# Five small moves in a fused sparse-attention and two-layer kernel: two matmul pieces, a deal of pieces, an order of sums, a split addition and a memset

## The chip, the cores and the metric

The kernel runs on one core of one Trainium2 chip. The metric is the device time of one execution in microseconds (us). The engines go by their short names: PE is TensorE, ACT ScalarE, DVE VectorE, POOL GpSimd, and SP is SyncE, which here only issues DMAs. Each engine works through its own list of instructions in order; semaphores order the engines among each other.

## The reference

Eight batches of eight heads, 576 positions, 64 columns per head. Heads 0 to 3 see the last 32 positions (local), heads 4 to 7 every position of the same remainder modulo 32 (strided). The attention output, 4608 rows of 512, goes through two layers.

```python
B, H, S, D = q.shape                                   # 8, 8, 576, 64
scores = scale * np.matmul(q, k.transpose(0, 1, 3, 2))
mask_local = (rel >= 0) & (rel < 32)                   # rel = query position - key position
mask_strided = (rel >= 0) & (pos[None, :] % 32 == pos[:, None] % 32)
scores = np.where(masks, scores, -1e9)                 # heads 0-3 local, 4-7 strided
attn = softmax(scores)
x = np.matmul(attn, v)  ->  [4608, 512]
h = x @ w_in                                           # [512, 2048]
g = np.maximum(h, 0.0) + alpha * np.minimum(h, 0.0)
out = g @ w_out                                        # [2048, 512]
```

## The kernel before, in words

**Attention.** Heads are handled in pairs, 32 in all: pairs 4b and 4b+1 are the local heads of batch b, 4b+2 and 4b+3 the strided ones. A pair goes through pieces: transposes of q and k (`T`, line 292), scores (`score_both`, `score_piece`: matmuls of lines 318 and 377, the exponential on ACT, lines 391 to 406, and a product with the mask on POOL or DVE, lines 397, 402 and 409), the product with v (`pv_piece`: matmuls of line 430, then on DVE a reciprocal and a product, lines 437 and 439), and a transposition of the result into xT, by PE and a copy (`x_piece`, line 455, copies of lines 230 to 234) or by a transposing DMA (`x_dma`, lines 469 and 472, with a copy on ACT, line 478). xT is a ring of 1536 columns with four blocks of 128 rows (kk): kk 0 and 1 hold the local pairs of a batch, kk 2 and 3 the strided ones.

**The two layers.** The 4608 rows are nine chunks of 512. The first layer of a chunk is 16 pieces (`lin1_piece`): four matmuls of 512 columns over kk (line 613), the negative part on ACT (`neg`, line 621), and the join with alpha on DVE (`gT`, line 624), which goes into a list `late` and is written out at the next step. The second layer of chunk 0 is plain: `U(kf)` are three matmuls of 512 columns (line 884), `W(i)` two (line 899), called a quarter piece here. The second layer of chunks 1 to 8 (`lin2_fast`) uses a scheme with seven products, named "1", "5", "6", "2", "7", "3", "4" in their order, on sums of blocks of g (`gsum`, line 653, on POOL or DVE) and of w_out (`wsum`, line 640); each has two parts of eight (or sixteen) matmuls of 256 columns (lines 709 and 719). Their accumulators lie in PSUM banks a, b, e and f; bank b takes products "6", "7" and "4" upon a copy of a. The results go out through `store` (copy on ACT, line 662, or addition on DVE, line 664, then a DMA from SP, line 668). The accumulators and the first layer's outputs share one pool of three PSUM buffers, used in turn.

**Order.** The program order is written out by hand and kept. It begins with loads, memsets and a list of pieces for batch 0 and chunk 0; then a second list (from line 913) mixes U and W with the pieces of batch 1. The scores of pairs 4 and 5 come in it as `sc1(4)` and `sc1(5)`. From then on a loop runs over the chunks n = 1 to 8 with 30 steps each, i = 0 to 15 for the first layer and i = 16 to 29 for the second. After each step `attn_n(cnt, ab)` deals out cnt attention pieces of the next batch. cnt comes from an accumulator that spreads the pieces left over the steps (half as densely in the first layer), except in chunk 1 and chunk 6, which have lists of steps of their own. The dictionaries `early`, `sums`, `sums2` say at which step a gsum is made and by which engine.

**Loads.** SP and ACT issue the first loads of q and k; POOL issues those of v and of the weights, which change the type on the way, through the software queue (q0 of the profile). `x16s` is a fixed tile of 80 rows for the strided pairs that are transposed by DMA; its last 16 rows are set to zero once.

Of the kernel before, what the change touches and what calls it, by code (L numbers as in the profile page):

```python
# [9 lines left out]
F32 = mybir.dt.float32  # L10
F16 = mybir.dt.float16
ALU = mybir.AluOpType
# [20 lines left out]
def kernel(  # L33
# [10 lines left out]
    nc = tc.nc  # L44
    keep = tc.keep_in_program_order
# [443 lines left out]
    def T(u, nm):  # L489
        return lambda: transpose_piece(u, nm)  # L490
# [110 lines left out]
    def lin1_piece(n, m, begin=False):  # L601
        if n not in gTs:
            gTs[n] = gpool.tile([128, 16, 512], F16, tag="gT", name="gT")
        c0 = (512 * n) % RING
        hps = begun.pop(m, None)
        if hps is None:
            pool, tag = (pspool, "ps") if n == 0 and m // 3 % 2 else (phpool, "hps")
            hps = pool.tile([128, 512], F32, tag=tag, name="hps")
            order = (0, 1, 2, 3) if n else (2, 3, 0, 1)
        else:  # L610
            order = (0, 1)
        for kk in order[0:2] if begin else order:
            keep(nc.tensor.matmul(  # L613
                hps, win16[:, kk, 128 * m : 128 * m + 128], xT[:, kk, c0 : c0 + 512],
                start=(kk == (0 if n else 2)), stop=(kk == (3 if n else 1))))
        if begin:
            begun[m] = hps
            return

        neg = npool.tile([128, 512], F32, tag="neg", name="neg")  # L620
        keep(nc.scalar.activation(neg, hps, AF.Relu, scale=-1.0))  # L621

        def fin():
            keep(nc.vector.scalar_tensor_tensor(  # L624
                gTs[n][:, m, :], neg, oma[:, m : m + 1], hps, op0=ALU.mult, op1=ALU.add))
        late.append(fin)
# [45 lines left out]
    def lin2_fast(n, i):  # L672

        last = n == NCH - 1
        x, r = (("1", i) if i < 2 else ("5", i - 2) if i < 4 else ("6", i - 4) if i < 6 else ("2", i - 6) if i < 8
                else ("7", i - 8) if i < 10 else ("3", i - 10) if i < 12 else ("4", i - 12))
        if last and i > 10:  # L680
            x, r = (("4", 0), ("4", 1), ("3", 1))[i - 11]
        b = {"1": "a", "2": "a", "5": "e", "3": "e"}.get(x, "b")
        first = x in "15" and r == 0
        if first:
            bank[b] = phpool.tile([128, 512], F32, tag="hps", name="ops")
        o = bank[b][:, 256 * r : 256 * r + 256]
        if last and b == "e" and r == 1:
            o = bank["f"][:, 0:256]

        def g(t, j):  # L690
            return lambda y: gTs[n][:, 2 * y + j, 256 * t + 128 * r : 256 * t + 128 * r + 128]

        def s(z):
            return lambda y: gsum[z][:, y, 128 * r : 128 * r + 128]

        def w(j, c):
            return lambda y: wout16[:, 2 * y + j, 256 * c : 256 * c + 256]

        def t(z):
            return lambda y: wsum[z][:, y, :]  # L700

        def both(h):
            if x == "5" and h == 0 and last:
                bank["f"] = pspool.tile([128, 512], F32, tag="ps", name="opsl")
            for z in range(2):
                i, alone = int(x) - 5, x == "5" and last and z == 1
                o = bank["f"][:, 0:256] if alone else bank[b][:, 256 * z : 256 * z + 256]
                for y in range(4 * h, 4 * h + 4):
                    keep(nc.tensor.matmul(  # L709
                        o, gsum[i][:, y, 128 * z : 128 * z + 128], wsum[i][:, y, :],  # L710
                        start=(x == "5" and y == 0 and (z == 0 or alone)), stop=(y == 7), skip_group_check=True))

        lhs, rhs = {
            "1": (g(0, 0), w(0, 0)), "2": (g(0, 1), w(1, 0)), "3": (s(3), w(1, 1)),
            "4": (g(1, 1), t(3)), "5": (s(0), t(0)), "6": (s(1), t(1)), "7": (s(2), t(2))}[x]
        if x in "56":
            both(r)
        for y in range(0 if x in "56" else 8):
            keep(nc.tensor.matmul(  # L719
                o, lhs(y), rhs(y), start=(first and y == 0), stop=(y == 7), skip_group_check=True))  # L720
        if last and x == "3":
            store(n, 0, 1, bank["f" if r else "e"], bank["s6"], r)
            return
        if last and x == "5" and r:
            bank["s5"] = npool.tile([128, 512], F32, tag="par", bufs=2, name="par")
            for z, o in enumerate((bank["e"], bank["f"])):
                keep(nc.scalar.copy(bank["s5"][:, 256 * z : 256 * z + 256], o[:, 0:256]))
            return
        if r == 0:
            return  # L730
        if x == "1":
            bank["b"] = phpool.tile([128, 512], F32, tag="hps", name="ops")
            keep(nc.scalar.copy(bank["b"], bank["a"]))
        elif x in "56":
            z = npool.tile([128, 512], F32, tag="par", bufs=2, name="par")
            keep(nc.scalar.copy(z, bank[b]))  # L736
            bank["s" + x] = z
        elif x == "2":
            store(n, 0, 0, bank["a"])
        elif x == "7":  # L740
            late.append(lambda: store(n, 1, 1, bank["b"], bank["s5"]))
        elif x == "3":
            late.append(lambda: store(n, 0, 1, bank["e"], bank["s6"]))
        else:
            store(n, 1, 0, bank["b"])
# [40 lines left out]
    keep(nc.vector.memset(kTs[0][:, :, 608:672], 0.0))  # L786
    for nm in "qk":
        keep(nc.vector.memset(qks[nm][64:80], 0.0))
    keep(nc.vector.memset(x16s[64:80], 0.0))
    keep(nc.vector.tensor_copy(id32, ident[0:72, 0:72]))  # L790

    keep(nc.gpsimd.memset(vss[0][:, :, :, 64:65], 1.0))
# [30 lines left out]
    def ov(b, eng, c0, c1):  # L823
        return lambda: over_v(b, eng, c0, c1)
# [82 lines left out]
    def ws(z):  # L907
        return lambda: wout_sum(z, "dve", 0)

    def sc1(g, eng="dve"):  # L910
        return lambda: score_both(pairs[g], eng)

    for fn in [
        vs(1, 0, "pool"), sc1(6), U(0), vs(1, 1, "pool"), U(1), sc1(7), U(2), U(3), Cl(1, "q", "act"), Pv(6, 1),
        Cl(1, "k"), Pv(6, 2), Pv(6, 0), U(4), U(5), Pv(7, 0), Pv(7, 1), U(6), loads2, T(2, "q"), U(7), Pv(7, 2), W(0), W(1),
        T(2, "k"), ws(0), ws(1), ws(2), W(2), sc1(4), U(8), W(3), ov(1, "dve", 0, 24), U(9), sc1(5, "pool"), W(4), U(10), X(7, "act"), U(11),
        X(6, "act"), Pv(4, 1), W(5), Cl(2, "q", "act"), Cl(2, "k", "act"), U(12), Pv(4, 0), U(13), Pv(5, 0), U(14), Pv(5, 1),
        U(15), W(6), X(4, "dve"), X(5, "dve"), W(7)]:
        fn()
# [18 lines left out]
    for n in range(1, NCH):  # L938
        ab = attn_until(n + 1) if n + 1 < B else len(pieces)
        left = ab - pos["i"]  # L940
        acc = 0.0
        for i in range(30):
            if i < 16:
                lin1_piece(n, 8 * (i // 8) + 2 * (i % 4) + i % 8 // 4)
            else:
                lin2_fast(n, i - 16)
            held = []
            if n == 1 and i == 15:
                held.extend(late)
                late.clear()  # L950
            if n == 6:
                cnt = int(i in (2, 5, 7, 9, 16, 17, 19, 20, 22, 24, 25, 27))
            elif n == 1:
                cnt = int(i > 12 or i in (0, 2, 4, 6, 9, 11))
            else:
                acc += left / (19.5 if n == B - 2 else 21) * (0.5 if i < 16 else 1.0)
                cnt = int(acc)
                acc -= cnt
            attn_n(cnt, ab)
            for fn in held:  # L960
                fn()
            if n == 2 and i == 8:
                load_v(4, True)
            for z, h, eng in {1: early, 2: sums2}.get(n, sums).get(i, ()):
                g_sum(n, z, h, eng)
            if n > 1:
                continue
            if i == 7:
                for pr in range(2):
                    cast_v(2, pr, "pool")  # L970
                    load_qk(4, "qk"[pr])
            if i == 4:
                load_v(3, True)
            if i == 15:
                load_v(3, False)
                load_d(3)
                cast_l(3, "q", "act")
            if i == 17:
                cast_l(3, "k", "act")
            if i == 24:  # L980
                for pr in range(2):
                    cast_v(3, pr, "pool")
        while pos["i"] < ab:
            attn_step(ab)
# [30 lines left out]
```

## Time and profile before

| | before |
|---|---|
| median of 3 runs | 297.91 us (297.36 to 298.34) |
| the profiled execution | 296.76 us |
| its span, first to last instruction | 294.9 us |
| granted TensorE clock | 1.000 |
| PE busy | 289.3 us (98%) |
| DVE busy | 216.1 us (73%) |
| ACT busy | 182.1 us (62%) |
| POOL busy | 181.7 us (62%) |
| HBM read, written | 38.24 MB, 9.44 MB |

A row of the timeline reads: start and duration in us, engine, line, operation, output <- inputs, shapes, xcount, and in brackets the idle time of the engine before it and what ended that. Rows of one line in a stretch are merged, and the duration is that of the merged row. PE's matmuls overlap: each is shown some 0.16 us longer than the step from one to the next. Line numbers are those of the kernel before.

### The profile page before, as it was taken

What the parts mean: (1) busy time and instruction counts of PE and PEld (TensorE: products, weight loads), DVE (VectorE), ACT (ScalarE), POOL (GpSimd) and SP (SyncE); (2) the same over time, 40 slices, a digit from 0 to 9 for tenths busy, and PEclk for the clock granted to TensorE, in tenths of its full rate; (3) what the DMA queues carried; (4) which work ended last, traced back from release to release, by engine and by line L of the source; (5) the groups of instructions that cost most, each with busy time, mean ns of one, the idle gap of its engine ahead of it and who ended that gap; (6) DMA issues with size and microseconds to landing.
All of it is one profiled execution on the core that took longest, in us unless ns stands there. A gap on an engine that the chain in (4) does not pass through costs nothing.

```text
span 294.9 us, 6948 instructions
## 1 busy us (share of the span) xinstructions
PE 289.3 (98%) x2732; PEld 187.3 (64%) x2732; DVE 216.1 (73%) x412; ACT 182.1 (62%) x337; POOL 181.7 (62%) x167
## 2 busy tenths in 40 slices
PE   8999999999999999999999999999999999999995
PEld 3764554545885488547864786478646864784584
DVE  5688876579966895689668975897489948927851
ACT  1777756797957864775477537754776266417630
POOL 8462547999589997889897985777364105002200
PEclk9999999999999999999999999999999999999999
DMA  7999999999999999999999999976411230021004
GB/s 180 263 194 203 239 212 258 221 158 336 114 110 196 153 151 129 195 136 153 174 185 146 122 144 194 134 115 117 150 20 23 58 109 0 0 87 58 2 0 143
DMA packets 97488, 41.18 MB, mean 140 GB/s; under 512 B 75360, under 2 KB 94256, under 8 KB 97456
## 3 DMA queue, kind: packets, MB, share of 16 engines
q0 software_dynamic: 51008, 17.77, 59.7%
q1 hardware_dynamic: 46096, 22.32, 37.2%
q10 hardware_dynamic: 352, 0.66, 0.9%
q8 instruction: 21, 0.34, 0.5%
q14 instruction: 11, 0.09, 0.1%
HBM read 38.24 MB, written 9.44 MB: 162 GB/s over the span
## 4 chain that ended last, share of the span: by engine, by line
PE 91%; DVE 3%; DMA 2%; issue 2%; ACT 1%; SPq 0%; DVEq 0%; ACTq 0%
PE hps L613 41%; PE ops L719 22%; PE ops L709 8%; PE pv L430 5%; PE ops L884 4%; PE sp L377 2%; DMA consts<-consts 2%; PE tp L292 1%; PE xp L455 1%; PE sph L377 1%; PE ops L899 1%; DVE gT L624 1%; PE tf L154 1%; DVE gsum L653 1%; PE wps L761 1%
## 5 line engine op out<-in xcount | busy, mean ns | idle before, releaser
L613 PE MATMUL hps<-xT,win 128*128 128x512 f16 x576 | 132.9, 379 | 0.1
L624 DVE SCALAR_TENSOR_TENSOR gT<-neg,oma,hps 128x512 f16<-128x512 f32 x144 | 105.2, 744 | 36.2 <-ACT neg L621 28.6
L621 ACT ACTIVATE neg<-hps 128x512 f32<-128x512 f32 x144 | 85.8, 598 | 34.6 <-PE hps L613 32.4
L613 PEld LDWEIGHTS <-win 128*128 128x128 f16 x576 | 53.3, 98 | 58.3 <-issue 0.8
L653 POOL TENSOR_TENSOR gsum<-gT 128x1024 f16<-128x1024 f16 x15 | 31.8, 2123 | 37.6 <-DVE gT L624 37.5
L402 POOL TENSOR_TENSOR et<-et,consts 128x576 f16<-128x576 f16 (+1 forms) x23 | 32.1, 1394 | 34.7 <-ACT et L400 34.4
L719 PEld LDWEIGHTS <-gT 128*128 128x128 f16 x384 | 35.7, 98 | 6.1 <-issue 0.5
L439 DVE TENSOR_TENSOR x<-pv,rc 96x384 f16<-96x384 f32 (+2 forms) x62 | 33.0, 532 | 2.1
L719 PE MATMUL ops<-wout,gT 128*128 128x256 f16 x256 | 32.1, 273 | 0.0
L709 PE MATMUL ops<-wsum,gsum 128*128 128x256 f16 x248 | 30.7, 273 | 0.2 <-DVE gsum L653 0.2
L409 POOL TENSOR_TENSOR et<-et,consts 128x576 f16<-128x576 f16 (+1 forms) x23 | 29.7, 1290 | 0.1
L430 PEld LDWEIGHTS <-et 72*128 72x128 f16 (+1 forms) x448 | 23.6, 98 | 8.4 <-ACT et L339 0.4
L709 PEld LDWEIGHTS <-gsum 128*128 128x128 f16 x256 | 23.6, 98 | 3.3 <-DVE gsum L653 0.4
L719 PEld LDWEIGHTS <-gsum 128*128 128x128 f16 x256 | 23.7, 98 | 2.9
L400 ACT ACTIVATE et<-sp 128x576 f16<-128x576 f32 (+1 forms) x24 | 15.5, 645 | 16.4 <-PE sp L377 16.4
L664 DVE TENSOR_TENSOR osb<-ops,par 128x512 f32<-128x512 f32 (+1 forms) x16 | 10.7, 674 | 17.1 <-PE ops L719 9.4
L437 DVE RECIPROCAL rc<-pv 72x6 f32<-72x6 f32 (+2 forms) x80 | 14.7, 183 | 10.2 <-PE pv L430 9.8
L662 ACT COPY osb<-ops 128x512 f32<-128x512 f32 x16 | 9.4, 587 | 16.8 <-PE ops L719 16.7
L406 ACT ACTIVATE et<-sph 128x288 f16<-128x288 f32 (+1 forms) x48 | 18.9, 409 | 0.0
L736 ACT COPY par<-ops 128x512 f32<-128x512 f32 x15 | 8.8, 587 | 13.1 <-PE ops L709 12.6
L719 PE MATMUL ops<-wsum,gT 128*128 128x256 f16 x128 | 16.1, 273 | 0.3 <-DVE osb L664 0.3
L719 PE MATMUL ops<-wsum,gsum 128*128 128x256 f16 x128 | 16.1, 272 | 0.0
(112 smaller groups left out, 354.5 us busy)
## 6 DMA issues: line engine op xcount, KB each, us to landing
out_dram<-osb SPq DMA_DIRECT2D x35, 256.0 KB, 3.0
vl<-in_v_dram POOLq DMA_DIRECT2D x6, 384.0 KB, 9.7
win<-in_moe_w_in_dram POOLq DMA_DIRECT2D x4, 512.0 KB, 17.4
wout<-in_moe_w_out_dram POOLq DMA_DIRECT2D x4, 512.0 KB, 17.1
qsd<-in_q_dram POOLq DMA_DIRECT2D x7, 288.0 KB, 7.5
ksd<-in_k_dram POOLq DMA_DIRECT2D x7, 288.0 KB, 8.8
stv<-in_v_dram POOLq DMA_DIRECT2D x7, 288.0 KB, 7.7
ql<-in_q_dram SPq DMA_DIRECT2D x3, 576.0 KB, 8.8
```

Source lines behind the costliest of these rows:

```text
L400: keep(nc.scalar.activation(ev.rearrange("r (y c) -> r y c", y=2), sp[0:r, :, 0:n], AF.Exp, scale=SCALE))
L402: keep(mul(mv, mv, m, op=ALU.mult))
L406: keep(nc.scalar.activation(ev[:, n * y : n * y + n], sps[y][0:r, 0:n], AF.Exp, scale=SCALE))
L409: keep(mul(mv, mv, m, op=ALU.mult))
L430: keep(nc.tensor.matmul(pv[:, 65 * x : 65 * x + 65], et[0:r, c : c + 128], v16[0:r, 2 * P.pr + hh, t, :] if P.strided else v16[:, 6 * (2 * ...
L439: keep(nc.vector.tensor_tensor(P.x16[0:w, c0 : c0 + 64 * nb].rearrange("r (c e) -> r c e", e=64), pvv[:, :, 0:64], rc[0:w, 0:nb].unsqueeze ...
L613: keep(nc.tensor.matmul(hps, win16[:, kk, 128 * m : 128 * m + 128], xT[:, kk, c0 : c0 + 512], start=(kk == (0 if n else 2)), stop=(kk == ( ...
L621: keep(nc.scalar.activation(neg, hps, AF.Relu, scale=-1.0))
L624: keep(nc.vector.scalar_tensor_tensor(gTs[n][:, m, :], neg, oma[:, m : m + 1], hps, op0=ALU.mult, op1=ALU.add))
L653: keep((nc.vector if eng == "dve" else nc.gpsimd).tensor_tensor(gsum[i][:, hs], a, b, op=op))
L709: keep(nc.tensor.matmul(o, gsum[i][:, y, 128 * z : 128 * z + 128], wsum[i][:, y, :], start=(x == "5" and y == 0 and (z == 0 or alone)), st ...
L719: keep(nc.tensor.matmul(o, lhs(y), rhs(y), start=(first and y == 0), stop=(y == 7), skip_group_check=True))
```

## The change

Five edits, all in the order or place of work; the same matmuls are made.

1. In the second list, `W(3)` moves from behind `U(8)` to ahead of `sc1(4)`, the scores of pair 4.
2. Chunk 6 loses its own list of steps: cnt comes from the accumulator as in chunks 2 to 5. The pieces of its first layer then come at steps 3, 6, 9 and 12 instead of 2, 5, 7 and 9 (in the order: pair 28's second product with v, pair 30's scores, pair 29's two products with v); those from step 16 on stay.
3. `lin1_piece` of chunk 1 sums over kk in the order 2, 3, 0, 1, as chunk 0 does.
4. In the last chunk, product "7" adds its result and s5 in two halves of 256 columns, at once instead of through `late`, with one store for both.
5. The memset of the last 16 rows of `x16s` moves from DVE, as its last but one instruction ahead of the first loads' use, to POOL, ahead of the memsets and DMAs that POOL begins with.

```diff
-            order = (0, 1, 2, 3) if n else (2, 3, 0, 1)
+            order = (0, 1, 2, 3) if n > 1 else (2, 3, 0, 1)
...
-                start=(kk == (0 if n else 2)), stop=(kk == (3 if n else 1))))
+                start=(kk == (0 if n > 1 else 2)), stop=(kk == (3 if n > 1 else 1))))
...
+        elif x == "7" and last:
+            osb = opool.tile([128, 512], F32, tag="osb", name="osb")
+            for z in range(2):
+                c = slice(256 * z, 256 * z + 256)
+                keep(nc.vector.tensor_tensor(osb[:, c], bank["b"][:, c], bank["s5"][:, c], op=ALU.add))
+            keep(nc.sync.dma_start(
+                out[512 * n + 256 : 512 * n + 512, 256:512].rearrange("(r p) c -> p r c", p=128),
+                osb.rearrange("p (r c) -> p r c", r=2)))
         elif x == "7":
             late.append(lambda: store(n, 1, 1, bank["b"], bank["s5"]))
...
-    keep(nc.vector.memset(x16s[64:80], 0.0))
+    keep(nc.gpsimd.memset(x16s[64:80], 0.0))
...
-        T(2, "k"), ws(0), ws(1), ws(2), W(2), sc1(4), U(8), W(3), ov(1, "dve", 0, 24), U(9), ...
+        T(2, "k"), ws(0), ws(1), ws(2), W(2), W(3), sc1(4), U(8), ov(1, "dve", 0, 24), U(9), ...
...
-            if n == 6:
-                cnt = int(i in (2, 5, 7, 9, 16, 17, 19, 20, 22, 24, 25, 27))
-            elif n == 1:
+            if n == 1:
```

More of the change, by code (lines that the diff above doesn't have):

```diff
@@ L915 @@
         Cl(1, "k"), Pv(6, 2), Pv(6, 0), U(4), U(5), Pv(7, 0), Pv(7, 1), U(6), loads2, T(2, "q"), U(7), Pv(7, 2), W(0), W(1),
-        T(2, "k"), ws(0), ws(1), ws(2), W(2), sc1(4), U(8), W(3), ov(1, "dve", 0, 24), U(9), sc1(5, "pool"), W(4), U(10), X(7, "act"), U(11),
+        T(2, "k"), ws(0), ws(1), ws(2), W(2), W(3), sc1(4), U(8), ov(1, "dve", 0, 24), U(9), sc1(5, "pool"), W(4), U(10), X(7, "act"), U(11),
         X(6, "act"), Pv(4, 1), W(5), Cl(2, "q", "act"), Cl(2, "k", "act"), U(12), Pv(4, 0), U(13), Pv(5, 0), U(14), Pv(5, 1),
```

## The prediction

> **What bounds the kernel now.** I read the page first, then the chain that ended last, then each engine's timeline wherever TensorE (PE) stands still for longer than its own matmuls explain. The page and two pieces of the chain:
>
> ```profile
> span 294.9 us, 6948 instructions
> PE 289.3 (98%) x2732; PEld 187.3 (64%) x2732; DVE 216.1 (73%) x412; ACT 182.1 (62%) x337; POOL 181.7 (62%) x167
> ...
> PE 91%; DVE 3%; DMA 2%; issue 2%; ACT 1%; SPq 0%; DVEq 0%; ACTq 0%
> ...
> 72.72 0.87 PE ops L719 x8
> ...
> 88.98 2.59 PE hps L613 x12
> ```
>
> PE is busy for 98% and carries 91% of the chain. Back to back, a 512-column matmul takes 2.59 / 12 = 0.216 us and a 256-column one 0.87 / 8 = 0.109. The change adds and removes no matmul. So it can gain only where PE starts a matmul later than these steps allow, and since PE is dense elsewhere, a hole closed anywhere should move the end by its size. The edits meet five such places.
>
> **The two quarter pieces** (W(3), two 512-column matmuls) move ahead of pair 4's scores. PE and VectorE (DVE) there:
>
> ```profile
> 44.39 0.59 PE L899 MATMUL ops<-wout,gT 128*128 128x512 f16 x2
> 45.46 0.30 PE L377 MATMUL sp<-qT,kT 64*128 64x96 f16 x6 [0.47 <-DVE kT L232]
> ...
> 44.59 0.72 DVE L232 COPY kT<-tp 128x512 f16<-128x512 f16 x1 [0.73 <-PE tp L292]
> ```
>
> W(2) leaves PE free at 44.39 + 2 x 0.216 = 44.82, but the scores start at 45.46, when the copy of kT has ended: a hole of 0.64 (the row's 0.47 counts from the modelled end of the matmul). W(3) is 0.43 of work and needs nothing that W(2) lacked. It fits into the hole, the scores start at 45.46 as before, and everything behind them is 0.43 earlier. The copy hangs on transposes issued before W(2), so nothing is queued behind a new wait. Bounds: 0 to -0.43; I take **-0.43**, for the hole is larger than the work.
>
> **Chunk 1, strided heads first.** The next line-613 group is its first:
>
> ```profile
> 55.44 0.73 PE L613 MATMUL hps<-xT,win 128*128 128x512 f16 x2
> ...
> 54.92 0.82 DVE L232 COPY xT<-xp 128x576 f16<-128x576 f16 x2
> ```
>
> Two matmuls took 0.73, against 0.59 for the two at 44.39: 0.14 more, as the second needs pair 5's xT, copied until 55.74. With kk 2 and 3 first, the local heads are needed 0.43 later, and the copies cover that. Bounds 0 to -0.18; I take **-0.14**.
>
> These 0.57 must survive until chunk 2, where ScalarE (ACT) waits for a transposing DMA:
>
> ```profile
> 87.19 1.40 ACT L478 COPY xT<-xs 128x384 f16<-128x384 f16 x2 [0.16 <-DMA xs<-x16s]
> 88.50 0.69 ACT L230 COPY xT<-xp 128x384 f16<-128x384 f16 x2
> ...
> 88.81 2.75 PE L613 MATMUL hps<-xT,win 128*128 128x512 f16 x12
> ```
>
> PE needs the last copy (ended 89.19) for its fourth matmul, at 88.81 + 3 x 0.216 = 89.46: slack 0.27. If that DMA lands 0.57 earlier like its issuers, nothing is lost: **0**. If it stays where it is, 0.57 - 0.27 = 0.30 comes back; that is the upper bound.
>
> **Chunk 6 by the accumulator.** Pair 28's last piece moves from step 2 to 3, pair 30's scores from 5 to 6, pair 29's pieces from 7 and 9 to 9 and 12; from step 16 on all is equal.
>
> ```profile
> 219.21 5.63 PE L613 MATMUL hps<-xT,win 128*128 128x512 f16 x24
> ...
> 229.89 0.29 PE L430 MATMUL pv<-vs,et 72*128 72x65 f16 x4
> 230.41 1.05 PE L709 MATMUL ops<-wsum,gsum 128*128 128x256 f16 x8 [0.23 <-DVE gsum L653]
> ...
> 226.90 1.76 DVE L653 TENSOR_TENSOR gsum<-gsum,gT 128x1024 f16<-128x1024 f16 x1
> ...
> 229.28 1.07 DVE L653 TENSOR_TENSOR gsum<-gsum,gT 128x1024 f16<-128x1024 f16 x1
> ...
> 226.78 1.34 POOL L402 TENSOR_TENSOR et<-et,consts 72x576 f16<-72x576 f16 x1 [3.74 <-ACT et L400]
> ```
>
> At the usual pace 24 matmuls take 2.75 + 12 x 0.216 = 5.34; here 5.63. The 0.29 is PE waiting for a PSUM buffer, because DVE, given pair 29's two pieces only two steps apart, falls behind with gT. Three steps apart it does not: chunk 5 deals so, and shows what is late next:
>
> ```profile
> 190.82 0.35 PE L430 MATMUL pv<-vl,et 128*128 128x65 f16 x6
> ...
> 193.05 1.39 DVE L624 SCALAR_TENSOR_TENSOR gT<-neg,oma,hps 128x512 f16<-128x512 f32 x2
> ...
> 200.77 1.28 DVE L653 TENSOR_TENSOR gsum<-gT,gsum 128x1024 f16<-128x1024 f16 x2
> ...
> 201.04 2.15 POOL L402 TENSOR_TENSOR et<-et,consts 128x576 f16<-128x576 f16 x1 [3.93 <-ACT et L400]
> ```
>
> There the gT behind the piece ends at 193.05 + 0.69 = 193.74, 2.92 after the piece's matmuls began, and frees a PSUM buffer some 0.1 later. In chunk 6 the first second-layer group wants that buffer 6 x 0.03 + 12 x 0.216 = 2.77 after them: a new hole of 0.25 at step 16 (chunk 5 has pair 27's scores in between, chunk 6 not). So -0.29 + 0.25.
>
> The second hole: the four 65-column matmuls at 229.89, each 65/256 of 0.109, 0.03, end at 230.01, and PE goes on at 230.41: 0.40, for gsum(1,1). DVE is late because a gsum that meets a mask product of GpSimd (POOL) takes 1.76 and 1.07 instead of 1.28 / 2 = 0.64. In chunk 5 the same pair met, DVE had started first, and POOL took 2.15. Whoever starts first keeps its pace. At 226.78 POOL was 0.12 ahead of the gsum at 226.90. The new hole delays pair 31's scores, and with them the mask, by 0.25, but not the gsum: now DVE is first by 0.13, gsum(1,1) ends about 1 us sooner, and the hole goes: -0.40. If the order holds as it was, 0.40 - 0.25 = 0.15 stays. Bounds of this edit: 0 (both holes as before) to -0.69 (no new one); I take **-0.44**.
>
> **The last chunk's addition in halves.**
>
> ```profile
> 287.62 1.04 PE L719 MATMUL ops<-wout,gsum 128*128 128x256 f16 x8
> 288.98 1.91 PE L719 MATMUL ops<-wsum,gT 128*128 128x256 f16 x16 [0.32 <-DVE osb L664]
> ...
> 237.23 0.69 DVE L664 TENSOR_TENSOR osb<-ops,par 128x512 f32<-128x512 f32 x1 [0.58 <-PE ops L719]
> ...
> 288.23 1.02 DVE L664 TENSOR_TENSOR osb<-ops,par 128x512 f32<-128x512 f32 x2 [4.03 <-issue]
> 291.85 0.42 DVE L664 TENSOR_TENSOR osb<-opsl,par 128x256 f32<-128x256 f32 x1 [2.60 <-PE opsl L719]
> ```
>
> PE could go on at 287.62 + 8 x 0.109 = 288.49 and goes on at 288.98: 0.49, because "4" adds into the bank that this addition reads. If half the bank were released after the first half, 0.69 - 0.42 = 0.27 would be won. But in the built program the first half raises no semaphore, the second raises it by 2, and PE's one wait, ahead of "4"'s first half, stands at the count that the second reaches. So PE waits for both. The addition at 288.23 and the 256-column one behind it take 1.02 together, so the second starts 1.02 - 0.42 = 0.60 after the first, 0.09 before its 0.69 is over; two halves end after (0.42 - 0.09) + 0.42 = 0.75, 0.06 later than one: **+0.06**. [...] Bounds: -0.27 to +0.16 (twice 0.42 less 0.69, rounded up). The store follows the second half in either case and lies well ahead of the end.
>
> **The memset of x16s on POOL** stands ahead of all DMAs that POOL issues:
>
> ```profile
> 0.79 0.22 POOL L793 MEMSET vl<- 32x64 f16 x1
> ...
> 1.41 1.55 POOL L212 DMA_DIRECT2D stv<-in_v_dram  x2 [0.25 <-issue]
> ...
> 84.62 2.02 POOL L234 COPY vs<-stv 72x1024 f16<-72x1024 f16 x2
> ...
> 4.49 0.48 DVE L789 MEMSET x16s<- 16x512 uint32 x1
> 6.89 0.19 DVE L790 CAST id<-consts 72x72 f32<-72x72 f16 x1 [1.92 <-DMA consts<-consts]
> 10.12 0.43 DVE L232 COPY vs<-stv 72x1024 f16<-72x1024 f16 x1 [0.32 <-DMA stv<-in_v_dram]
> 10.65 0.46 DVE L232 CAST qT<-tf 128x288 f16<-128x288 f32 x1
> ...
> 11.47 0.30 PE L318 MATMUL sp<-qT,kT 64*128 64x72 f16 x8
> ...
> q10 hardware_dynamic: 291, 0.56, 37.9%
> q1 hardware_dynamic: 321, 0.46, 33.2%
> ...
> q0 software_dynamic: 9, 0.01, 5.4%
> ```
>
> DVE gains nothing: it waits 1.92 for the constants. For POOL the trace has no memset of 1024 columns: 0.22 for 64 columns is the floor, 2.02 for two copies of 1024 makes 1.01 each, twice that the ceiling; I take 1.0. Every issue of POOL, v first, then the weights, is then 1.0 later. The last three rows are the DMA queues in the first 6 us (the first two) and in the seventh: POOL's queue, issued to from 1.41, moved nothing in 6 us while two others shared the engines, and 9 packets in the next. An issue at 2.4 is still well ahead, so the v load lands when it did: **0**. Ceiling: the full delay D, in the rivals.
>
> **Sum.** -0.43 - 0.14 - 0.44 + 0.06 = -0.95. The profiled execution took 296.76, 1.86 more than its span; it becomes 295.8. The median of the runs, 297.91, is 1.15 above it; the same step gives **297.0**.
>
> **Rivals.** (1) The v load moves with its issue, D = 1.0. The copy at 10.12 and, in order behind it, the cast of qT (free to start at 10.65, DVE busy until 10.55 + D) slide; the cast ends at 12.01, the scores of pair 3 start at 12.05 instead of 11.47: +0.58, 297.5. For it: between 10.1 and 11.5 nothing has more slack than the 0.42. Against: the queue rows. [...] Chance 0.15. (2) **Slower**: the same place with a memset at its ceiling, D = 2.0 or more: each further us of D adds 1 us, so the price is D - 0.42. It eats the 0.95 from D = 1.4, at 2.0 it gives 298.5, and passes +0.3% at D = 2.3. Chance 0.09. (3) The transposing DMA of chunk 2 does not move: +0.30, 297.3; for it, ACT's wait at 87.19; against, that all that issues it hangs on PE. Chance 0.13. (4) The halves do release the bank early: -0.33 against the sum, 296.6; chance 0.07. The forecast has 0.56.
>
> A measurement of this kernel tells about 0.3%, 0.89 us, from no change, so faster begins at 297.0: the forecast lies on that edge. Its unknown ends lean outward (no new hole in chunk 6, -0.25), and case 4 lies beyond; I give faster 0.50, same 0.44, slower 0.06. The range: the largest gains together, -0.43 - 0.18 - 0.69 - 0.27, reach 296.3; upwards it takes in cases 1 and 3 and half the spread of the runs shown (0.4), but only part of case 2: 296.2 to 298.3.
>
> **What would show it.** The scores of pair 4 with a hole near 0.2 instead of 0.64; two matmuls in 0.59 at the head of chunk 1; 24 matmuls of chunk 6 without the 0.29, a hole of 0.25 ahead of its first L719 group, gsum at 0.7 beside a longer mask; near 0.55 ahead of the last sixteen L719; the v copy still at 10.1. Wrong it is if that copy moves to 11, if chunk 2's first matmuls spread beyond 2.75, or if the gsums of chunk 6 stay at 1.76.

## The result, and the profile after

| | before | after |
|---|---|---|
| median, 14 runs each | 297.33 us | 296.38 us |
| fastest | 296.98 | 295.57 |
| ratio of after to before, 95% interval | | 0.9967 [0.9952, 0.9982] |
| profiled execution, its span | 296.76, 294.9 | 297.99, 296.2 |

The median fell by 0.95, the sum forecast. It stands at 296.4 and not at the 297.0 named, because the forecast started from three runs of before with a median of 297.91; the fourteen here have 297.33. But the profiled execution of after is one of its three longest: it is *longer* than that of before, and shows both what the edits won and what is lost in some executions. (Runs in a disturbed state are left out of the ratios; the profiles of three experiments, e1, e8 and e13, have a mean clock of 0.994, and of these only distances between neighbouring instructions are used.)

The page of after, lines on the span and the chain:

```profile
span 296.2 us, 6949 instructions
...
PE 80%; DMA 11%; DVE 4%; POOL 2%; ACT 2%; issue 1%; SPq 0%; DVEq 0%; ACTq 0%; POOLq 0%
...
PE hps L613 38%; PE ops L719 20%; PE ops L709 8%; DMA win<-in_moe_w_in_dram 5%; PE ops L892 4%; DMA kT<-ksd 4%; PE pv L430 3%; DMA xs<-x16s 2%; PE sp L377 2%; DVE gsum L653 1%; PE ops L907 1%; PE tp L292 1%; PE sph L377 1%; PE xp L455 1%; D
```

The chain was 2% DMA before and is 11% now: three loads end waits that PE did not have. First the places of the edits, PE unless marked (lines behind 739 are 8 further down than before, those behind 953 6):

```profile
45.08 1.03 PE L907 MATMUL ops<-wout,gT 128*128 128x512 f16 x4
46.15 0.30 PE L377 MATMUL sp<-qT,kT 64*128 64x96 f16 x6
...
55.68 1.03 PE L613 MATMUL hps<-xT,win 128*128 128x512 f16 x4
...
223.72 2.75 PE L613 MATMUL hps<-xT,win 128*128 128x512 f16 x12
226.54 1.03 PE L719 MATMUL ops<-wout,gT 128*128 128x256 f16 x8
...
231.74 0.29 PE L430 MATMUL pv<-vs,et 72*128 72x65 f16 x4
231.87 1.04 PE L709 MATMUL ops<-wsum,gsum 128*128 128x256 f16 x8
...
228.60 0.69 DVE L653 TENSOR_TENSOR gsum<-gsum,gT 128x1024 f16<-128x1024 f16 x1
...
228.63 1.79 POOL L402 TENSOR_TENSOR et<-et,consts 72x576 f16<-72x576 f16 x1 [4.91 <-ACT et L400]
...
289.08 1.04 PE L719 MATMUL ops<-wout,gsum 128*128 128x256 f16 x8
290.20 1.91 PE L719 MATMUL ops<-wsum,gT 128*128 128x256 f16 x16
...
289.33 0.81 DVE L744 TENSOR_TENSOR osb<-ops,par 128x256 f32<-128x256 f32 x2 [3.67 <-issue]
```

Pair 4's scores start 0.21 behind W(3) (45.08 + 4 x 0.216 = 45.94). Four matmuls at the head of chunk 1 take 1.03, so none of them waits. In chunk 6 the first-layer matmuls run without a stall, a hole of 0.23 stands ahead of the first second-layer group (223.72 + 12 x 0.216 = 226.31), and none ahead of the line-709 group (four steps of 0.03 from 231.74). The gsum that took 1.76 takes 0.69, 0.03 ahead of a mask product that now takes 1.79. The last hole is 0.25 (289.08 + 0.87 = 289.95), not 0.49. Won: 0.43 + 0.14 + 0.45 + 0.24 = 1.26 (the expectations below have 0.23 and 1.25).

Lost in this execution, PE and ACT:

```profile
19.35 0.36 PE L430 MATMUL pv<-vl,et 128*128 128x65 f16 x6
20.38 0.60 PE L613 MATMUL hps<-xT,win 128*128 128x512 f16 x2 [0.67 <-DMA win<-in_moe_w_in_dram]
...
71.09 0.30 PE L377 MATMUL sp<-qT,kT 64*128 64x72 f16 x8 [0.84 <-DMA kT<-ksd]
...
89.57 1.40 ACT L478 COPY xT<-xs 128x384 f16<-128x384 f16 x2 [1.53 <-DMA xs<-x16s]
...
89.81 1.12 PE L613 MATMUL hps<-xT,win 128*128 128x512 f16 x3
91.39 1.46 PE L613 MATMUL hps<-xT,win 128*128 128x512 f16 x6 [0.46 <-ACT xT L230]
```

The first weights cost 0.83, the transposing DMA of kT 0.90, that of xs 0.93 (91.39 less 89.81 + 3 x 0.216): 2.66 in all. Besides, PE's first transposes started 0.25 sooner (the cast of the constants is at 6.56 instead of 6.89), and 0.14 of that went into a wait for the first copy of v: 2.66 + 0.14 - 0.25 - 1.26 = 1.29, against 1.3 between the spans.

### The profile page after: what moved, and what is told of

Its sections match the earlier page's. It is cut to its first block, busy times and chain, and to the rows that moved or that the text cites. A ratio compares the mean times of both kernels' runs of the same rounds, so it can differ in the third digit from the quotient of the medians.

```text
span 296.2 us, 6949 instructions
## 1 busy us (share of the span) xinstructions
PE 289.4 (98%) x2732; PEld 187.5 (63%) x2732; DVE 215.2 (73%) x412; ACT 182.3 (62%) x337; POOL 183.1 (62%) x168
## 3 DMA queue, kind: packets, MB, share of 16 engines
q0 software_dynamic: 51008, 17.77, 60.5%
## 4 chain that ended last, share of the span: by engine, by line
PE 80%; DMA 11%; DVE 4%; POOL 2%; ACT 2%; issue 1%; SPq 0%; DVEq 0%; ACTq 0%; POOLq 0%
PE hps L613 38%; PE ops L719 20%; PE ops L709 8%; DMA win<-in_moe_w_in_dram 5%; PE ops L892 4%; DMA kT<-ksd 4%; PE pv L430 3%; DMA xs<-x16s 2%; PE sp L377 2%; DVE gsum L653 1%; PE ops L907 1%; PE tp L292 1%; PE sph L377 1%; PE xp L455 1%; DVE gT L624 1%
## 5 line engine op out<-in xcount | busy, mean ns | idle before, releaser
L664 DVE TENSOR_TENSOR osb<-ops,par 128x512 f32<-128x512 f32 (+1 forms) x15 | 10.1, 674 | 13.1 <-PE ops L719 9.4
```

## The experiments

Theory A: the edits are worth their holes, and the memset on POOL delays the loads. Theory B (the prediction): the memset costs nothing. Besides, the last hole had to be explained, which shrank though the rows priced two halves above one addition. All kernels were timed in five rounds against the kernel before, which had medians of 297.45 (e1 to e4), 297.21 (e9, e5, e10, e11) and 297.24 (e8, e12, e13, e15).

**e1: after, memset back on DVE.**
```diff
-    keep(nc.gpsimd.memset(x16s[64:80], 0.0))
+    keep(nc.vector.memset(x16s[64:80], 0.0))
```


> The changed kernel with the memset of x16s back on DVE. Theory A (the memset on POOL delays the whole software queue: first issue 0.55 later, and each weight load lands 0.4 to 1.1 later, 0.90 for the first): the four other edits are worth 1.25 together (0.43 + 0.14 + 0.45 + 0.23 by the two traces), the first w_in load lands near 19.4 again, PE does not wait for it, and the median is 1.1 to 1.4 below the kernel before, 0.2 to 0.4 below the changed kernel. Theory B (the prediction: the memset costs nothing, the waits for loads in the profile of the changed kernel are chance): the same time as the changed kernel, 0.95 to 1.0 below the kernel before.

Measured: 296.74, ratio 0.9981 [0.9957, 1.0004]: 0.71 below before by the medians, less than either theory had, though the interval takes in both. POOL's first issue is at 1.41 and the first w_in lands at 19.36 again, as A says, but the last hole came back, larger:

```profile
292.05 1.04 PE L719 MATMUL ops<-wout,gsum 128*128 128x256 f16 x8
293.47 1.91 PE L719 MATMUL ops<-wsum,gT 128*128 128x256 f16 x16 [0.38 <-DVE osb L744]
...
292.66 0.76 DVE L744 TENSOR_TENSOR osb<-ops,par 128x256 f32<-128x256 f32 x2 [4.03 <-issue]
```

The hole is 293.47 - 292.92 = 0.55. DVE idled 4.03, as in the kernel before, and 3.67 in after: the addition starts 0.36 later behind the same matmuls. With the memset back on DVE that idle time is back too. The halves themselves take 0.76, the 0.75 predicted.

**e2: before, memset on POOL.** The reverse edit.

> The kernel before with only the memset of x16s on POOL. Theory A: POOL issues the v load at 1.95 instead of 1.41, the first w_in load lands at 20.0 to 20.4 instead of 19.43, later than the 19.64 at which PE wants it, and the median is 0.2 to 0.7 above the kernel before. Theory B: no difference, within 0.15.

Measured: 296.90, 0.9988 [0.9972, 1.0005]: 0.36 below before by the ratio, and not above, as A had it. The profile has w_in at 19.62 (A: 20.0 to 20.4), no wait for it, and the last hole at 0.13, 0.35 less than before: of a cost of the memset nothing is seen. The span of the profile is that of before even so, for PE starts its first transposes at 7.51 instead of 7.14: the dummy matmuls ahead of them (line 761) go over from steps of 0.43 to steps of 0.22 only near 6.6, in before near 5.4.

**e3: before, chunk 6 by the accumulator.**

> The kernel before with only chunk 6 dealt by the accumulator. The prediction's step: the hole of 0.29 among the 24 matmuls and the one of 0.40 ahead of the line-709 group go, one of 0.25 comes ahead of the first line-719 group: 0.44 faster. Rival: the gsum keeps meeting the mask product (the order DVE first is chance), 0.15 stays: 0.04 faster. The addition of the last chunk is unchanged here: if its late start of 0.40 after the semaphore belongs to that instruction, it is here again and PE waits 0.59 - 0.11 = 0.48; if it is chance, near 0.1.

Measured: 296.97, 0.9995 [0.9973, 1.0017]. The profile shows the step itself as forecast:

```profile
223.23 2.75 PE L613 MATMUL hps<-xT,win 128*128 128x512 f16 x12
226.05 1.03 PE L719 MATMUL ops<-wout,gT 128*128 128x256 f16 x8
...
231.25 0.29 PE L430 MATMUL pv<-vs,et 72*128 72x65 f16 x4
231.38 1.04 PE L709 MATMUL ops<-wsum,gsum 128*128 128x256 f16 x8
```

No stall, a hole of 0.23 at 226.05, none at 231.38. Its median is 0.48 below, its fastest execution 0.45 (296.31 against 296.76); its slow half (to 298.75) blurs the ratio. PE waited for xs in its profile too, 1.2 at the head of chunk 2. The last hole is 0.48 here.

**e4: after, single addition.**
```diff
-        elif x == "7" and last:
-            ...
```


> The changed kernel with the single addition for product 7 in the last chunk, as before. Theory S (the single addition, queued by late, starts 0.40 after its semaphore for a reason that belongs to its place, and the halves got rid of that): the hole ahead of the last sixteen line-719 matmuls is 0.48 again and the time is 0.23 above the changed kernel. Theory H (the halves cost 0.12, for DVE needs 0.81 instead of 0.69; the late start is chance or belongs to the kernel's layout): the hole is 0.13 and the time 0.12 below the changed kernel.

Measured: 296.04, 0.9956 [0.9932, 0.9981]; the fastest execution, 295.14, is the shortest of all runs.

```profile
288.88 1.04 PE L719 MATMUL ops<-wout,gsum 128*128 128x256 f16 x8
289.88 1.91 PE L719 MATMUL ops<-wsum,gT 128*128 128x256 f16 x16
...
289.14 1.24 DVE L664 TENSOR_TENSOR osb<-ops,par 128x512 f32<-128x512 f32 x2 [3.67 <-issue]
```

The hole is 0.13: theory H. The halves cost 0.12 in after, and the single addition is not late by itself. Counted over all of DVE's instructions in the trace, its waits for semaphores included, the late one is the 448th: the addition in before, e1 and e3, but in e2 and e4 a semaphore wait behind it, which starts 0.39 and 0.41 after the addition where it is 0.04 in before; nobody needs that one. Hence theory P.

**e9: before, one DVE instruction more.**
```diff
-    keep(nc.vector.memset(x16s[64:80], 0.0))
+    keep(nc.vector.memset(x16s[64:80, 0:512], 0.0))
+    keep(nc.vector.memset(x16s[64:80, 512:1024], 0.0))
```


> The kernel before with one DVE instruction more near its start: the memset of x16s in two halves of 512 columns, both on DVE. Nothing else is changed. Theory P (position: the late start of 0.36 to 0.41 falls on whatever instruction is DVE's 448th in the trace; in the kernel before that is the addition of the last chunk, in the changed kernel it is the second half): the 448th is now a gsum some 4 us ahead of anyone's need, the addition is the 449th, starts within 0.05 of its semaphore, the hole ahead of the last sixteen line-719 matmuls is 0.13 instead of 0.48, and the time is 0.35 below the kernel before. Theory W (the late start belongs to this addition's wait, which had lasted over 4 us): the hole stays at 0.48 and the time is that of the kernel before.

Measured: 296.83, 0.9980 [0.9964, 0.9997].

```profile
288.36 1.24 DVE L664 TENSOR_TENSOR osb<-ops,par 128x512 f32<-128x512 f32 x2 [3.67 <-issue]
...
288.10 1.04 PE L719 MATMUL ops<-wout,gsum 128*128 128x256 f16 x8
289.10 1.14 PE L719 MATMUL ops<-wsum,gT 128*128 128x256 f16 x9
```

The hole is 0.13: theory P. One more instruction, for the same work, is worth 0.35 at the other end of the program. In all 14 profiles, the first addition of the last chunk is late where it is the 448th (before, e1, e3, e5) and prompt where it is the 447th or 449th. The same addition of the chunk ahead, DVE's 420th to 422nd, idles 3.67 or 3.68 in every profile: that is the prompt value. Here the 448th is a gsum 4 us ahead of the addition.

**e5: before, W(3) and chunk 1's order alone.**

> The kernel before with only W(3) moved ahead of the scores of pair 4 and chunk 1 summed strided heads first. The prediction: -0.57, no give-back. Theory G (give-back: the transposing DMAs of kT near 70 and of xs near 88 land when the DMA engines let them, not earlier by 0.57): the two holes close (0.64 to 0.21, 0.14 to 0), PE waits for kT<-ksd or xs instead in the profile, and the median is 0.1 to 0.4 below the kernel before, while the fastest executions show the full 0.57.

Measured: 296.79, 0.9991 [0.9977, 1.0004]: 0.42 by the medians, at theory G's upper end, 0.27 by the ratio, the interval wide. The fastest execution, 296.23, is only 0.13 below the fastest of before (296.36), where theory G had the full 0.57. Both holes are closed; PE does not wait for kT, but ACT waits for xs:

```profile
87.85 1.40 ACT L478 COPY xT<-xs 128x384 f16<-128x384 f16 x2 [1.45 <-DMA xs<-x16s]
...
89.68 1.67 PE L613 MATMUL hps<-xT,win 128*128 128x512 f16 x7 [0.46 <-ACT xT L230]
```

The transposing DMA of xs was issued at 80.72, 0.64 sooner than in before, and landed at 87.83, 0.66 later. PE's wait at the head of chunk 2 is 0.86, more than both edits had won.

**e10: after, single addition, memset behind the w_in issues.**

> The changed kernel with the single addition for product 7 in the last chunk and with the memset of x16s on POOL behind the issues of the four w_in loads instead of ahead of all its DMAs. DVE keeps one instruction less than the kernel before, so the addition is its 447th. Theory P with a memset that does cost: all gains (0.43 + 0.14 + 0.45 + 0.35 = 1.37), the first issue of POOL at 1.41 again, 1.2 to 1.5 below the kernel before. If the memset's place costs nothing, the same as the changed kernel with the single addition, which was 1.3 below at a ratio of 0.9956.

Measured: 296.23, 0.9974 [0.9955, 0.9994]. POOL issues at 1.42 and w_in lands at 19.43, yet it is no better than e4, and 0.98 below before by the medians falls short of the 1.2 to 1.5 expected. In its profile PE waits 0.51 for kT and 1.83 for xs: these waits do not need the memset ahead of POOL's loads.

**e11: that, with v issued first.**

> The previous kernel (single addition, memset of x16s behind the w_in issues) with POOL's two loads of the strided heads' v issued ahead of its three small memsets. Theory A (POOL's first issue sets when the whole software queue lands): first issue near 0.75 instead of 1.41, the w_in and ksd loads land 0.4 to 0.9 earlier, fewer waits for kT<-ksd and xs, and the median is 0.2 to 0.6 below the previous kernel. Rival (the DMA engines are full from 3 us on and the other queues share them, so an earlier issue only changes who is served first): within 0.15 of the previous kernel.

Measured: 296.11, 0.9965 [0.9938, 0.9992]. It does not decide the question: the first issue came at 1.32, only 0.10 earlier, behind 0.88 of idle that the profile puts to POOL's own sequencer, and the memsets now stood ahead of the weights, whose issue went from 4.75 to 5.38 and landing from 19.43 to 19.91. PE waited 0.49 for them.

**e8: after, memset made twice.**

> The changed kernel with the memset of x16s made twice on POOL, one behind the other, ahead of its DMAs: 0.95 more, POOL's first issue near 2.9 instead of 1.95. Rival 1 and 2 of the prediction (the loads move with their issue, each us beyond the slack is paid): 0.9 above the changed kernel. The prediction's step (an issue at 2.4, and so perhaps at 2.9, is still ahead of when the queue moves): the same as the changed kernel. Between them, by what was measured so far (w_in landed 0.2 to 0.9 later for an issue 0.53 to 0.63 later): the first w_in load lands at 20.3 to 21.0, PE waits 0.6 to 1.3 for it, the median is 0.3 to 0.9 above the changed kernel.

Measured: 298.01, 1.0031 [1.0011, 1.0051]: 1.7 above after, each measured against its own runs of before, for 0.94 of memset. POOL, DVE, PE of its profile:

```profile
0.73 0.94 POOL L797 MEMSET x16s<- 16x1024 f16 x1 [0.29 <-POOLq L1006]
1.73 0.94 POOL L798 MEMSET x16s<- 16x1024 f16 x1
...
2.95 1.56 POOL L212 DMA_DIRECT2D stv<-in_v_dram  x2
...
11.82 0.89 DVE L232 COPY vs<-stv 72x1024 f16<-72x1024 f16 x1 [2.01 <-DMA stv<-in_v_dram]
...
12.86 0.34 PE L430 MATMUL pv<-vs,et 72*128 72x65 f16 x6 [1.48 <-DVE vs L232]
```

It was not w_in that paid: that landed at 19.34. The v load moved with its issue, and PE waited 1.65 longer for its copy than in before. That is the place of rivals 1 and 2. The price is above their 1:1 here for two reasons. The copy itself took 0.89 instead of 0.43. And the granted clock fell: from 14.8 to 18.1, 2 us behind that wait, it is 0.50 in the profile, and nine 128-column transposes take 1.17 (at 17.12), where they take 0.67 elsewhere (before, at 43.89). Seven of the twelve executions have a mean clock of 0.989 or 0.994, with a median of 298.75; the five with 0.998 or more have 297.15, which is 0.86 above after, each again measured against its own runs of before, and so near 1:1 (which five kept the clock need not be chance: their wait may have been the shorter one).

**e12: e4, batch 2's strided q and k loaded ahead of its v.**
```diff
-        load_v(2, False)
         load_d(2)
+        load_v(2, False)
```


> The changed kernel with the single addition, and with batch 2's loads of the strided q and k issued on POOL ahead of its load of the local heads' v instead of behind it. Theory G (PE's wait for kT<-ksd near 70 is the end of a chain of loads: ksd lands near 60, its transposing DMA near 70.5): ksd is issued 1.4 earlier, lands 1 to 2 earlier, the transposing DMA of kT is issued and lands earlier, PE does not wait there, and the profiled execution is 0.6 to 1.0 below the one of the kernel with the single addition; the median up to 0.4 below. Rival (the transposing DMA lands late because of the traffic around 60 to 70, whenever it is issued): PE waits 0.6 or more at 70 again.

Measured: 296.65, 0.9987 [0.9963, 1.0012]. ksd lands at 56.6 instead of 60.5, the transposing DMA of kT at 68.1 instead of 70.7, and PE waits neither there nor for xs. The profiled execution is 1.18 below that of e4, which was e4's longest, but the median is 0.61 above. Theory G holds for the mechanism, but not for the gain:

```profile
54.43 1.15 ACT L230 CAST kl<-kl 128x1152 f16<-128x1152 f32 x1 [1.77 <-DMA kl<-in_k_dram]
55.49 1.06 ACT L230 COPY osb<-ops 128x512 f32<-128x512 f32 x2
...
56.12 1.02 PE L613 MATMUL hps<-xT,win 128*128 128x512 f16 x4 [0.36 <-ACT osb L230]
```

Another load, kl, landed at 54.35 instead of 52.24 (in e13, with the same order, at 55.35); ACT waits for it, PE for the copies queued behind it, 0.53. PE paid here for a load that landed 2.11 later.

**e13: e12, batch 3's strided k loaded 7 steps later.**

> The previous kernel, and in chunk 1 the load of batch 3's strided k moved from step 15 to step 22, behind the mask products of POOL that come there, so that it is issued some 9 us later. Theory G2 (PE's wait of 0.3 to 2.2 for xs at the head of chunk 2 comes from the loads that the transposing DMA of xs shares the DMA engines with from 76 to 89): xs lands 1 to 2 earlier, near 87, and PE does not wait at the head of chunk 2; against that, the transposing DMA of kT of batch 3 comes some 3 later, with 5 in hand. 0.3 to 1.0 below the previous kernel. Rival (xs is late for another reason): the wait stays, no gain.

Measured: 304.72, 1.0246 [1.0225, 1.0267]: a failed experiment. In the order written the load now stands behind the transposing DMA that should read it, so batch 3's strided heads are scored with batch 2's k, and POOL waited with mask products queued behind it: that DMA landed at 91.74, and POOL issued the load at 92.42 (the row's name for what ended the wait is inferred). The wait for xs is gone; xs took 3.6 us from issue to landing, but in e12 it took 4.4 and nobody waited either. Theory G2 is not settled by it:

```profile
83.60 1.26 POOL L402 TENSOR_TENSOR et<-et,consts 128x576 f16<-128x576 f16 x1 [5.30 <-ACT et L400]
92.42 0.77 POOL L135 DMA_DIRECT2D ksd<-in_k_dram  x1 [7.56 <-PE hps L613]
```

**e15: e4 without the early edits.**

> The changed kernel with the single addition and without the two early edits: W(3) stays behind U(8), and chunk 1 sums local heads first; chunk 6's deal and the memset on POOL stay. If the early edits are worth their holes: 0.57 above the kernel with the single addition, 0.8 below the kernel before. If DMA waits take back most of it: 0.1 to 0.3 above the kernel with the single addition, 1.0 to 1.3 below the kernel before, and the profile shows no wait for kT<-ksd.

Measured: 296.26, 0.9965 [0.9951, 0.9978], from 296.01 to 296.49. Against e4 the early edits are then worth 0.22 by the plain medians, 0.43 by the medians each against its own runs of before, 0.27 by the ratios, and 0.87 between the fastest executions (295.14, 296.01). The intervals of the two ratios overlap almost wholly, so the two expectations are not told apart by the time. Its profile has no wait for a load. ACT's copies of xs:

```profile
86.95 1.41 ACT L478 COPY xT<-xs 128x384 f16<-128x384 f16 x2
```

Of the five profiles without the early edits (before, e2, e3, e9, e15) one, e3, has a wait at the head of chunk 2; the seven with them and batch 2's loads in their old order (after, e1, e4, e5, e8, e10, e11) all have one, of 0.45 to 2.9. That the early edits provoke it, and not chance alone, is likely but not shown, and how they would is open: xs is not only wanted earlier, it also landed later there (87.8 in e5 and e11, 89.3 to 91.4 in the other five, against 86.6 to 87.3 in before, e2, e9 and e15, and 89.05 in e3).

## Why the prediction was right, and where it was not

- **The total** was right: -0.95 forecast, -0.95 measured by the medians. It is the sum of terms that missed in both directions, so that it came out to the hundredth is luck; the interval of the ratio is 0.9 us wide.
- **W(3) and chunk 1**: -0.57, and the traces show both holes closed by that. The give-back was put at 0, with 0.30 as the bound and chunk 2 as the place. That is the step that failed. The profiled executions with both edits and the old order of loads wait there, for 0.45 to 2.9, and some also at pair 10's scores (kT<-ksd at 71.09), for 0.5 to 1.0. Chunk 2's first twelve matmuls spread over 3.68 in after (89.81 to 93.49), beyond the 2.75 that the prediction had named as a sign of being wrong. At the median some 0.15 (by the medians) to 0.30 (by the ratios) of the 0.57 is given back, in e5 as in e15 against e4, but the intervals do not exclude that nothing is. Rival 3 had the place, and put at most 0.30 on it. The argument that "all that issues it hangs on PE" took the issue for the landing: in e5 the issue came 0.64 sooner and the landing 0.66 later.
- **Chunk 6**: -0.44 forecast, 0.45 in after and in e3; the stall, the new hole of 0.23 for 0.25, and DVE's start ahead of POOL came as said, though by 0.03 and not 0.13.
- **The halves**: +0.06 forecast, with both halves waited for. The two take 0.76 in e1, where the late start falls ahead of both, 0.07 more than one: right. In after the 448th instruction is the second half, it starts 0.39 behind the first instead of 0.34, the two take 0.81 and cost 0.12. But the hole shrank by 0.24, since the prediction's working left 288.23 unexplained in the row it quoted: DVE could have started 0.35 sooner, and "[4.03 <-issue]" said that it waited for nothing shown. The late start went with the memset's place in DVE's list (e2, e4 and e9), which the sum had at 0. Why DVE's 448th instruction starts late is shown by no run here.
- **The memset**: 1.0 forecast, 0.95 measured. "Every issue of POOL is then 1.0 later" failed:

```profile
0.73 0.95 POOL L797 MEMSET x16s<- 16x1024 f16 x1 [0.29 <-POOLq L1005]
...
1.95 1.56 POOL L212 DMA_DIRECT2D stv<-in_v_dram  x2
...
10.53 0.43 DVE L232 COPY vs<-stv 72x1024 f16<-72x1024 f16 x1 [0.98 <-DMA stv<-in_v_dram]
```

The first issue is 0.54 later, because the 0.25 of idle ahead of it went and the small memsets overlap it. "An issue at 2.4 lands when it did" failed too: the first v load lands at 10.10 for an issue at 1.41, at 10.51 for 1.95, at 11.79 for 2.95 (e8). Over all profiles it lands at 10.24 to 10.83 in the six with one memset ahead and at 10.04 to 10.25 in the seven with none. So rival 1 had the mechanism and the wrong D; the slack of 0.42 that it named covered the 0.41, but for the 0.14 that PE waited because it was early (0.45 is lost there in e4, nothing in e2, e12 and e15). The wait of 0.83 for w_in in after is not shown to come from the memset: in the other five profiles with one memset ahead w_in lands at 19.38 to 19.62, and in e8 at 19.34. This load lands 8.3 to 8.9 behind its issue (8.7 in before, 8.6 in after, 8.8 in e8), so the delay passed on (0.41 of 0.54 in after, 1.69 for 1.54 in e8). The queue rows were no evidence against it.

The version with most gain here is e4, the change without its halves, at 0.9956; its interval overlaps that of the change, so that it is better is shown by the profile alone (0.13 against 0.25 at the last hole).

## What to carry to other kernels

An idle time that the profile puts down to "issue" is a term too: explain it before pricing the instruction behind it, and look whether the edit shifts that instruction's place in its engine's list (here 4.03 of idle became 3.67, a hole of 0.48 one of 0.13). A hole closed on a dense engine may be given back at the next transfer that does not move with it (in e5's profile 0.57 was closed and PE then waited 0.86), so give the landing of each later transfer its slack and its spread, not only its issue. An instruction ahead of the first loads of a queue can cost: its price here was near its delay less the slack at the landing, and that was found by doubling it (one memset, a delay of 0.54 against a slack of 0.42: nothing to be seen in e2; the second, 1.00 more: 0.86 above after at a full clock in e8). A wait on the matmul engine can cost more than its length: look at the granted clock behind it before putting a price on it (0.50 for 3.3 us behind the wait in e8).

## What the hardware showed that was not expected

- DVE's 448th instruction in the trace starts 0.39 to 0.42 behind the one ahead of it (the start of an addition, or the end of a wait) in 13 of 14 profiles, be it an addition, a second half or a wait; a wait starts 0.04 behind an addition otherwise (before), a second half 0.34 (e1). In e9, a gsum among gsums, it shows no delay. Moving one memset moved this off the path (a last hole of 0.48 in before, 0.13 in e2).
- Two executions of one kernel at a full clock differ by 2.4 us (after: 295.57 to 298.02, e3: 296.31 to 298.75) and more (before, beside e1 to e4: 296.76 to 299.57). The profiled ones that are long mostly have waits for transposing DMAs: xs took 4.4 us from issue to landing in e12, 5.2 in e15, 5.8 in before, 7.2 in after, 9.1 in e1.
- The granted clock of TensorE is 0.50 for 3.4 us in three profiles: from 14.8 in e8, from 92.9 in e1, from 114.5 in e13, each during or within 2 us behind a PE wait of 1.48 us or more (as the profile counts it). With the memset made twice, which lengthens the wait at 12.9, 7 of 12 executions have a mean clock of 0.994 or less, with it made once (after) 1 of 14. A wait of 1.95 in e13, at 57.1, had no such stretch behind it, so what sets it off is open.
- A POOL issue 1.54 later than in before (e8) delayed the landing of the first v load by 1.69, but not that of the first w_in load (19.34 against 19.43), 3.3 us of issues behind it.
